# Queries that reach the scores' operands by DMA transpose alone, in a fused windowed attention and MLP kernel

## The chip, the core and the metric

The kernel runs on one core of a Trainium2 chip. The core has five engines with instruction streams of their own: TensorE (PE in the profile; its weight loads are PEld), VectorE (DVE), ScalarE (ACT), GpSimd (POOL) and SyncE (SP), which here only issues DMAs. Sixteen DMA engines move what is issued. On-chip memory has 128 partitions; PE reads it and writes to a separate accumulator memory (PSUM), which POOL does not read here.

The metric is the device time of one execution in microseconds (us), median over runs. The profile shows one execution, whose span runs from the first to the last instruction.

## The reference

Attention with a window of 32 positions to each side, for 8 batches of 8 heads, 576 positions of 64 numbers, followed by two matrix products with a leaky ReLU between them:

```python
B, H, S, D = q.shape                                   # 8, 8, 576, 64
scores = (1.0 / np.sqrt(D)) * np.matmul(q, k.transpose(0, 1, 3, 2))
mask = np.abs(pos[:, None] - pos[None, :]) <= 32
scores = np.where(mask, scores, -1e9)
attn = np.exp(scores - np.max(scores, axis=-1, keepdims=True))
attn = attn / (np.sum(attn, axis=-1, keepdims=True) + 1e-09)
o = np.matmul(attn, v)
x = o.transpose(0, 2, 1, 3).reshape(B * S, H * D)      # 4608 x 512
h = x @ w_in                                           # 512 x 2048
g = np.maximum(0.01 * h, h)
out = g @ w_out                                        # 2048 x 512, float32
```

All inputs and the output are float32; the kernel works in bfloat16 inside.

## The kernel before

**Tiling.** Heads are taken in pairs: a pair's two heads of 64 numbers fill the 128 partitions. There are 4 pairs a batch. Queries and keys must stand with the 64 numbers of a head along the partitions, so each pair's block of 96 partitions (positions) by 768 columns (6 runs of positions, 2 heads, 64 numbers) is cast to bfloat16 and transposed.

**Two ways through the attention.** Batches 0 and 1 (`BY_DMA = 2`) are transposed on PE (`transposes`, L321 to L346), 16 steps in all. Batches 2 to 7 are transposed by DMA (`transpose_dma`, L302): the queries into a tile `kT` and the keys straight into the scores' operand `kz`. The scores of these batches take a block of 128 keys and the queries of both heads at once (`score_blocks`, L369 to L385), so each head's queries must stand in their own 64 partitions with zeros in the other 64. That padded operand is `qz`, two planes of 576 columns a pair. The zero halves are cleared once (`clear_q`, L228 to L237: on DVE for the even batches' set, on ACT for the odd ones'), and `place_queries` (L314 to L319) copies each head's half from `kT` into its plane on DVE, two copies a pair, three steps after the cast.

**Memory.** Two sets (`sets`, L152) serve even and odd batches from 2 on; each holds `qz`, `kz` and `vw`, the values with columns of ones beside them, so that the product that weights the values also gives the sums (`product_blocks`, L387). `set_ones` (L239 to L252) writes the ones on DVE and zeroes two corners a pair on POOL. In batches 0 and 1 the same memory holds other operands, `qT`, `kbd`, `vbd`.

**Steps.** One call of `step` (L587) is one step of the attention: the scores two steps ahead (PE), their exponential (ACT, L382) and the band mask (POOL, L384, which writes `prob`), then `weighted`: the product of this step (PE, L395), two copies to `r` (ACT, L402 and L403), the reciprocal (DVE, L404) and the scaling into `xT` (DVE, L408). After that come the chores due: casts of queries and keys on POOL (`cast_qk`, L285), their transposes on SP (L305), casts of the values on POOL (`cast_vw`, L298 to L300), loads of the values (L116) and of the next batch's queries and keys (`load_qk`, L82 and L87), all issued on SP.

Steps 16 to 71 take four blocks of 64 positions of one pair; nine blocks make a batch. `base(b)` is the step at which batch b's scores are first used: 16, 24, 32, 40, 52 and 60. The scores themselves are made two steps before. Pair p of batch b is cast and transposed at step `base(b) + p - 7`, placed at `base(b) + p - 4`, and pair p of batch b + 1 is loaded at `base(b) + p - 4`. A pair's float32 tile has one buffer, so a load waits for the cast of the batch before.

**What sets the order.** The kernel's order is written out by hand. From step 8 on a list of due times (L766 to L776) puts the steps between the tiles of the two matrix products: `h_tile` (L500, out through ACT at L514) and `o_tile` (L549, out through ACT at L554 and a store on SP at L555). Every engine runs its instructions in the order in which the program issues them, and SP's queue holds loads, transposes and stores in that same order.

Of the kernel before, what the change touches and what calls it, by code (L numbers as in the profile page):

```python
# [10 lines left out]
BF16 = mybir.dt.bfloat16  # L11
AF = mybir.ActivationFunctionType
# [4 lines left out]
def kernel(  # L17
# [15 lines left out]
    nc = tc.nc  # L33

    B, H, S, D = q.shape
    W = 32
# [4 lines left out]
    NPAIR = H // 2  # L41
# [101 lines left out]
    nc.vector.memset(ones_bd[64:128, 64:128], 1.0)  # L143


    qb = const.tile([96, NPAIR, RUN, 2, D], BF16)
    kb = const.tile([96, NPAIR, RUN, 2, D], BF16)

    KPAD = S + 2 * W
    N_Q, N_K, N_V, N_BD = NPAIR * 2 * S, NPAIR * KPAD, NPAIR * NB * 3 * D, NPAIR * NB * 128  # L150
    N_SET = N_Q + N_K + N_V
    sets = [const.tile([128, N_SET], BF16, name=f"set{i}") for i in range(2)]  # L152
    qT, kbd, vbd, qz, kz, vw = [], [], [], [], [], []
    for t, at in zip(sets, (0, N_SET - NPAIR * S)):
        qT.append(sets[0][:, at:at + NPAIR * S].rearrange("p (n s) -> p n s", n=NPAIR))
# [27 lines left out]
        [((4, 0, 32), (6, 32, 64), (8, 96, 48)), ((5, 0, 64), (7, 64, 64))],  # L183
    ]

    win = const.tile([128, 2, 3, 64], BF16)
    nc.gpsimd.memset(win, 1.0)
    for lo in (0, 64):
        w = win[lo:lo + 64]
# [14 lines left out]
        lo = (16, 0)[hf]  # L204
        nc.gpsimd.tensor_copy(out=mask[hf][:, 1, :, lo:lo + 128], in_=win_f[:, :, 0:128])

    band = const.tile([128, 8, 2, 32], BF16)

    def make_band():

# [11 lines left out]
        yield  # L222

    band_parts = make_band()
    one = const.tile([128, 1], BF16)
    nc.vector.memset(one, 1.0)

    def clear_q(i, pairs, eng):  # L228
        for p in pairs:
            for a in range(2):  # L230
                r = slice(64 * (1 - a), 64 * (1 - a) + 64)
                if eng is nc.scalar:
                    eng.activation(
                        out=qz[i][r, p, a], in_=zero[r].to_broadcast([64, S]), func=AF.Copy)
                else:
                    eng.memset(qz[i][r, p, a], 0.0)
                yield  # L237

    def set_ones(i, pairs, eng):  # L239

        for p in pairs:
            to = vw[i][:, p, :, 1]
            if eng is nc.scalar:
                eng.activation(
                    out=to, in_=one.to_broadcast([128, NB * D]).rearrange("p (m d) -> p m d", d=D),
                    func=AF.Copy,
                )
            else:
                eng.memset(to, 1.0)
            nc.gpsimd.memset(vw[i][0:W, p, 0, 1], 0.0)  # L250
            nc.gpsimd.memset(vw[i][128 - W:128, p, NB - 1, 1], 0.0)
            yield  # L252

    def clear_k(i):
# [22 lines left out]


    def cast_qk(b, p, q_eng=None):
        for eng, src, dst in ((q_eng or nc.gpsimd, qf, qb), (nc.gpsimd, kf, kb)):  # L280
            to, tok = dst[:, p], src[b, p].rearrange("p a (c d) -> p c a d", d=D)
# [18 lines left out]
        nc.gpsimd.tensor_copy(out=to[64:128, 1::2, 0:3:2], in_=src[0:64, 1:5])  # L300

    def transpose_dma(b, p):  # L302
        t = kt.tile([128, S], BF16, name="kT")
        for to, src in ((t, qb), (kz[b % 2][:, p, W:W + S], kb)):
            nc.sync.dma_start_transpose(  # L305
                out=to.rearrange("p (c i) -> p c i", c=RUN),
                in_=src[:, p].rearrange("p c a d -> p (c a d)"),
            )
        landing.append((base(b) - 4 + p, b, p, t))

    def base(b):
        return OLD + NPAIR * (NB * (b - BY_DMA) // 4)

    def place_queries():  # L314
        while landing and landing[0][0] <= state["done"]:
            _, b, p, t = landing.pop(0)
            for a in range(2):
                r = slice(64 * a, 64 * a + 64)
                nc.vector.tensor_copy(out=qz[b % 2][r, p, a], in_=t[r])  # L319

    def transposes(b):  # L321

        for p in range(NPAIR):
            for which, src in (("q", qb), ("k", kb)):
                tp = mmps.tile([128, RUN, 96], BF16, name="tp", tag="mm")
                for c in range(RUN):
                    nc.tensor.transpose(  # L327
                        tp[:, c],
                        src[:, p, c].rearrange("p a d -> p (a d)"),
                        ident[0:96, 0:96],  # L330
                    )

                tok = tp.rearrange("p (e c) i -> p c i e", c=2)
                if which == "q":
                    nc.scalar.activation(
                        out=qT[b][:, p].rearrange("p (c i e) -> p c i e", c=2, e=RUN // 2),
                        in_=tok, func=AF.Copy,
                    )
                else:
                    kT = kt.tile([128, S], BF16, name="kT")  # L340
                    nc.scalar.activation(
                        out=kT.rearrange("p (i c) -> p i c", c=RUN),
                        in_=tp.rearrange("p c i -> p i c"), func=AF.Copy,
                    )
                    unplaced.append((b, p, kT))
                yield  # L346

    unplaced, landing = [], []

    def place_keys():  # L350

# [17 lines left out]
    def score_blocks(i):  # L369
        p, bs = i % NPAIR, blocks_of(i)  # L370
        n = 2 * 64 * len(bs)
        lo = 512 * (i % 2)
        sc = ps[:, lo:lo + n].rearrange("p (a w c i) -> p a w c i", a=2, c=2, i=32)
        for w, (b, m) in enumerate(bs):
            tok = qz[b % 2][:, p].rearrange("p a (g c i) -> p a g c i", c=2, i=96)
            at = 32 * (m % 3)
            nc.tensor.matmul(  # L377
                sc[:, :, w], kz[b % 2][:, p, 64 * m:64 * m + 128],
                tok[:, :, m // 3, :, at:at + 32], start=True, stop=True,
            )  # L380
# [200 lines left out]
    chores, more = [], []  # L581

    def chore(from_=chores):
        while from_ and next(from_[0], "end") == "end":
            from_.pop(0)

    def step():  # L587
        i = state["done"]
        if JOINED - 1 <= i < OLD - 1:
            join(i + 1)  # L590
        if i < NC - 2:
            score(i + 2)
        weighted(i)
        place_keys()
        place_queries()
        for b, p in qk_due.get(i, ()):
            cast_qk(b, p)
            transpose_dma(b, p)
        for b, p in v_due.get(i, ()):
            cast_vw(b, p)  # L600
        for b, p in v_next.get(i, ()):
            load_v_pairs(b, p)
        for b, p in qk_next.get(i, ()):
            load_qk(b, p)
        if i == 10:
            more.append(clear_q(1, range(NPAIR), nc.scalar))
        chore(more)
        if i == OLD - 2:
            chores.append(set_ones(0, (2, 3), nc.vector))
        if i == OLD:  # L610
            chores.extend([clear_k(1), set_ones(1, range(NPAIR), nc.vector)])
        if OLD - 6 <= i < OLD - 3:
            next(band_parts)
        chore()
        state["done"] += 1
# [95 lines left out]
    for f in range(4, FFC):  # L711
# [124 lines left out]
```

## Time and profile before

| | |
|---|---|
| median of 3 runs | 321.72 us (321.56 to 323.42) |
| the profiled execution | 321.12 us |
| its span | 319.4 us, TensorE clock granted in full |
| PE busy | 298.3 us |
| DVE busy | 227.3 us |
| ACT busy | 219.5 us |
| POOL busy | 200.1 us |
| DMA | 49.45 MB, mean 155 GB/s |
| L319, placing copies (DVE) | 48 of 487 ns, 23.4 us |
| L305, transposes (SP) | 48, of 1.2 us to issue (median) |

The page of the profile gives busy times, then the span in 40 slices of about 8 us, each digit the busy share in tenths. The list of waits says which engine waited at which line for whom: us in total, times, longest. The timeline gives instructions in order: start, duration, engine and line, operation, out<-in, count; "SPq" marks SP's issuing of DMAs, whose duration is the time to issue and not to land. A bracket at the end of a timeline row is idle time of the engine before it and what ended it. DMA shares count the packets' time against 16 engines, and go over 1 where packets of one engine overlap.

### The profile page before, as it was taken

The page shows a single profiled execution, that of the slowest core. Times are in us where ns is not written, and L with a number is a line of the kernel's source. Part 1 is how long each engine was busy: PE and PEld are TensorE (multiplying, and loading weights), DVE is VectorE, ACT ScalarE, POOL GpSimd, SP SyncE. Part 2 cuts the span into 40 slices and gives each one's busy share as a digit, 9 for nine tenths or more (in the row PEclk, how much of TensorE's full clock was granted, in tenths as well). Part 3 has the DMA queues.
Part 4 walks back from the last instruction along what each step waited for, and adds up shares of the span by engine and source line. Part 5 has one row for each costly group of instructions (what it writes and reads, how often), then busy time and mean ns, then how long its engine had stood idle before and what let it go on. Part 6 is the DMA issues. An engine that isn't in the chain of part 4 may idle for free.

```text
span 319.4 us, 6520 instructions
## 1 busy us (share of the span) xinstructions
PE 298.3 (93%) x2346; PEld 182.1 (57%) x2377; DVE 227.3 (71%) x299; ACT 219.5 (69%) x474; POOL 200.1 (63%) x262
## 2 busy tenths in 40 slices
PE   2678998999899899999999999999999999999995
PEld 1557774575665757676775555555555555544643
DVE  5688986899877997899779766787678766753000
ACT  7686689585865867776776975697569647842731
POOL 7899964997976987787677236678767722110000
PEclk9999999999999999999999999999999999999999
DMA  8999998998998699979969983699871011001001
GB/s 189 227 183 227 268 246 185 220 217 176 199 223 176 154 213 237 166 125 207 247 145 173 218 193 89 144 210 204 170 142 52 2 66 68 2 33 68 33 33 66
DMA packets 122416, 49.45 MB, mean 155 GB/s; under 512 B 96656, under 2 KB 117904, under 8 KB 122384
## 3 DMA queue, kind: packets, MB, share of 16 engines
q1 hardware_dynamic: 118160, 44.84, 68.5%
q0 software_dynamic: 4224, 4.19, 8.1%
q8 instruction: 18, 0.29, 0.4%
q14 instruction: 14, 0.11, 0.1%
HBM read 36.70 MB, written 9.44 MB: 144 GB/s over the span
## 4 chain that ended last, share of the span: by engine, by line
PE 76%; DVE 10%; ACT 5%; issue 4%; POOL 3%; DMA 1%; ACTq 0%; POOLq 0%; DVEq 0%
PE mm L549 34%; PE mm L500 32%; PE ps L377 3%; DVE r L404 2%; DVE set L319 2%; DVE r L451 2%; PE s L395 2%; PE x L395 1%; DVE xT L408 1%; DMA kT<-qb 1%; PE x L462 1%; PE ps L417 1%; PE tp L327 1%; PE s L446 1%; POOL prob L424 1%
## 5 line engine op out<-in xcount | busy, mean ns | idle before, releaser
L500 PE MATMUL mm<-xT,w_in_bf 128*128 128x288 bf16 (+3 forms) x824 | 134.7, 313 | 1.9 <-ACT gT L514 1.4
L549 PE MATMUL mm<-w_out_bf,gT 128*128 128x512 bf16 (+2 forms) x569 | 128.9, 373 | 1.3
L404 DVE RECIPROCAL r<-r 128x256 f32<-128x256 f32 (+1 forms) x56 | 95.0, 1696 | 37.7 <-ACT r L403 37.2
L500 PEld LDWEIGHTS <-w_in_bf 128*128 128x128 bf16 x832 | 79.0, 98 | 43.4 <-issue 2.9
L384 POOL TENSOR_TENSOR prob<-e,band 128x512 bf16<-128x512 bf16 (+1 forms) x56 | 62.7, 1119 | 63.1 <-ACT e L382 61.6
L514 ACT ACTIVATE gT<-mm 128x288 bf16<-128x288 f32 (+3 forms) x208 | 87.6, 469 | 15.7 <-PE mm L500 12.8
L549 PEld LDWEIGHTS <-gT 128*128 128x128 bf16 x592 | 55.0, 98 | 57.8
L382 ACT ACTIVATE e<-ps 128x512 bf16<-128x512 f32 (+1 forms) x56 | 32.5, 580 | 43.5 <-PE ps L377 35.8
L554 ACT ACTIVATE o_sb<-mm 128x512 f32<-128x512 f32 (+2 forms) x37 | 21.6, 585 | 24.1 <-PE mm L549 20.2
L451 DVE RECIPROCAL r<-s 128x288 f32<-128x288 f32 x16 | 31.2, 1951 | 4.4 <-PE s L446 4.0
L285 POOL CAST kb<-kf 96x768 bf16<-96x768 f32 x32 | 27.5, 862 | 4.1 <-DMA kf<-in_k_dram 4.0
L319 DVE COPY set<-kT 64x576 bf16<-64x576 bf16 x48 | 23.4, 487 | 3.9 <-DMA kT<-qb 3.1
L408 DVE TENSOR_TENSOR xT<-x,r 64x256 bf16<-64x256 f32 (+1 forms) x56 | 23.1, 413 | 3.3
L408 DVE TENSOR_TENSOR xT<-s,r 64x256 bf16<-64x256 f32 (+1 forms) x56 | 23.1, 413 | 3.3
L424 POOL TENSOR_TENSOR prob<-e,mask 128x576 bf16<-128x576 bf16 x16 | 20.4, 1274 | 7.3 <-ACT e L422 5.9
L377 PEld LDWEIGHTS <-set 128*128 128x128 bf16 x216 | 16.9, 98 | 13.0 <-issue 2.1
L377 PE MATMUL ps<-set 128*128 128x128 bf16 x216 | 22.0, 219 | 1.6 <-DVE set L319 1.5
L285 POOL CAST qb<-qf 96x768 bf16<-96x768 f32 x24 | 19.7, 821 | 0.0
L395 PEld LDWEIGHTS <-set 128*128 128x128 bf16 x432 | 17.9, 98 | 0.5
L298 POOL CAST set<-vbuf 128x640 bf16<-128x640 f32 x24 | 17.6, 732 | 0.0
L299 POOL CAST set<-vbuf 64x512 bf16<-64x512 f32 x24 | 14.7, 614 | 1.5
L300 POOL CAST set<-vbuf 64x512 bf16<-64x512 f32 x24 | 14.7, 612 | 1.2
(73 smaller groups left out, 220.6 us busy)
## 6 DMA issues: line engine op xcount, KB each, us to landing
qf<-in_q_dram SPq DMA_DIRECT2D x32, 288.0 KB, 5.3
kf<-in_k_dram SPq DMA_DIRECT2D x32, 288.0 KB, 6.1
out_dram<-o_sb SPq DMA_DIRECT2D x35, 256.0 KB, 2.5
vbuf<-in_v_dram SPq DMA_DIRECT2D x36, 128.0 KB, 4.4
vbuf<-in_v_dram SPq DMA_DIRECT2D x16, 144.0 KB, 6.2
vbuf<-in_v_dram SPq DMA_DIRECT2D x24, 96.0 KB, 4.1
w_in_bf<-in_moe_w_in_dram POOLq DMA_DIRECT2D x4, 512.0 KB, 8.5
w_out_bf<-in_moe_w_out_dram POOLq DMA_DIRECT2D x4, 512.0 KB, 16.4
```

The source lines that it names most:

```text
L285: eng.tensor_copy(out=to, in_=tok)
L319: nc.vector.tensor_copy(out=qz[b % 2][r, p, a], in_=t[r])
L377: nc.tensor.matmul(sc[:, :, w], kz[b % 2][:, p, 64 * m:64 * m + 128], tok[:, :, m // 3, :, at:at + 32], start=True, stop=True,)
L382: nc.scalar.activation(out=e[:, 0:n], in_=ps[:, lo:lo + n], func=AF.Exp, scale=scale)
L384: nc.gpsimd.tensor_mul(pr, e[:, 0:n], band.rearrange("p w c i -> p (w c i)")[:, 0:n])
L395: nc.tensor.matmul(x[:, a, w], vw[b % 2][:, p, m, a:a + 2].rearrange("p n d -> p (n d)"), pr[:, a, w], start=True, stop=True,)
L404: nc.vector.reciprocal(r[:, 0:n], r[:, 0:n])
L408: nc.vector.tensor_mul(xT[rows, p, t0:t0 + n], x[rows, a], r[rows, 0:n])
L451: nc.vector.reciprocal(r, s)
L500: nc.tensor.matmul(h[:, 0:n], w_in_bf[:, c, ts(f, 128)], xT[:, c, t0:t0 + n], start=(c == 0), stop=(c == DMC - 1),)
L514: nc.scalar.activation(out=to, in_=h, func=AF.Prelu, alpha=0.01)
L549: nc.tensor.matmul(o[:, lo:hi], gT[:, f, t0:t0 + 128], w_out_bf[:, f, lo:hi], start=(f == 0), stop=(f == FFC - 1),)
```

## The change

The queries of a pair are cast beside zeros. The buffer `qb` now has three slots instead of one place for each pair, and a slot has 1664 columns: head 0's six runs at columns 0 to 767, head 1's from 832 on, each run of 64 numbers followed or preceded by 64 columns of zeros. Seen as 12 blocks of 128 columns, the first six have head 0's numbers in the lower half and zeros above, the next six the reverse. One DMA transpose of 96x1536 then writes both padded planes of `qz`, zeros included. The slots are zeroed once (`clear_q`, six memsets on DVE: three in the second batch's first tiles, three at steps 9 to 11, since batches 0 and 1 use that part for plain casts).

Gone are `place_queries`, the clears of `qz`, the tile `kT` of the DMA's queries. Keys' casts have three slots too. Loads of pairs 2 and 3 come at `base(b) - 1` and `base(b) + 1` instead of `base(b) - 2` and `base(b) - 1`; as `base(b) + 1` is, for batches 2 to 4, also the step of the next batch's first transposes, pair 3's load now stands behind these in SP's queue. `set_ones` writes its corners on DVE, and for the first set all in the second batch's tiles. `qT` of batch 1 moves to the second set, the window's pattern and the band's mask into memory that is free at that time.

```diff
-    qb = const.tile([96, NPAIR, RUN, 2, D], BF16)
-    kb = const.tile([96, NPAIR, RUN, 2, D], BF16)
+    QB = 2 * RUN * 128 + 128
+    SLOTS = 3
+    qb = const.tile([96, SLOTS, QB], BF16)
+    kb = const.tile([96, SLOTS, RUN, 2, D], BF16)
+    qv = [
+        qb[:, p % SLOTS].rearrange("q (a x) -> q a x", a=2)[:, :, 0:RUN * 128]
+        .rearrange("q a (c e) -> q c a e", e=128)[:, :, :, 0:D]
+        for p in range(NPAIR)
+    ]
+    q01 = [
+        qb[:, p % SLOTS, 0:RUN * 128].rearrange("q (c a d) -> q c a d", a=2, d=D) for p in range(NPAIR)
+    ]
...
-        qz.append(t[:, 0:N_Q].rearrange("p (n a s) -> p n a s", n=NPAIR, a=2))
+        qz.append(t[:, 0:N_Q].rearrange("p (n s) -> p n s", n=NPAIR))
...
-    win = const.tile([128, 2, 3, 64], BF16)
+    win = sets[1][:, 0:384].rearrange("p (c m i) -> p c m i", c=2, i=64)
...
-    band = const.tile([128, 8, 2, 32], BF16)
+    band = mask[0].rearrange("p n c i -> p (n c i)")[:, 0:512].rearrange(
+        "p (w c i) -> p w c i", c=2, i=32)
...
-    def clear_q(i, pairs, eng):
...
+    def clear_q(p, a):
+        at = D if a == 0 else QB - 128 - RUN * 128
+        nc.vector.memset(
+            qb[:, p % SLOTS, at:at + RUN * 128].rearrange("q (c e) -> q c e", e=128)[:, :, 0:D], 0.0)
+
+    def set_ones(i):
+        for p in range(NPAIR):
+            nc.vector.memset(vw[i][:, p, :, 1], 1.0)
+            nc.vector.memset(vw[i][0:W, p, 0, 1], 0.0)
+            nc.vector.memset(vw[i][128 - W:128, p, NB - 1, 1], 0.0)
             yield
...
     def transpose_dma(b, p):
-        t = kt.tile([128, S], BF16, name="kT")
-        for to, src in ((t, qb), (kz[b % 2][:, p, W:W + S], kb)):
-            nc.sync.dma_start_transpose(
-                out=to.rearrange("p (c i) -> p c i", c=RUN),
-                in_=src[:, p].rearrange("p c a d -> p (c a d)"),
-            )
-        landing.append((base(b) - 4 + p, b, p, t))
+        nc.sync.dma_start_transpose(
+            out=qz[b % 2][:, p].rearrange("p (n i) -> p n i", i=96), in_=qb[:, p % SLOTS, 0:QB - 128],
+        )
+        nc.sync.dma_start_transpose(
+            out=kz[b % 2][:, p, W:W + S].rearrange("p (c i) -> p c i", c=RUN),
+            in_=kb[:, p % SLOTS].rearrange("p c a d -> p (c a d)"),
+        )
...
-    def place_queries():
-        while landing and landing[0][0] <= state["done"]:
-            _, b, p, t = landing.pop(0)
-            for a in range(2):
-                r = slice(64 * a, 64 * a + 64)
-                nc.vector.tensor_copy(out=qz[b % 2][r, p, a], in_=t[r])
...
-                qk_next.setdefault(base(b) + p - 4, []).append((b + 1, p))
+                qk_next.setdefault(base(b) + (-4, -3, -1, 1)[p], []).append((b + 1, p))
...
-        place_queries()
         for b, p in qk_due.get(i, ()):
+            if b == BY_DMA and p < SLOTS:
+                clear_q(p, 0)
             cast_qk(b, p)
             transpose_dma(b, p)
...
-        if i == 10:
-            more.append(clear_q(1, range(NPAIR), nc.scalar))
-        chore(more)
...
-    chores.extend([clear_q(0, range(NPAIR), nc.vector), clear_k(0),
-                   set_ones(0, (0, 1), nc.vector)])
+    chores.extend([clear_k(0), set_ones(0)])
...
+        if f < 4 + SLOTS:
+            clear_q(f - 4, 1)
```

More of the change, by code (lines that the diff above doesn't have):

```diff
@@ L153 @@
     qT, kbd, vbd, qz, kz, vw = [], [], [], [], [], []
-    for t, at in zip(sets, (0, N_SET - NPAIR * S)):
-        qT.append(sets[0][:, at:at + NPAIR * S].rearrange("p (n s) -> p n s", n=NPAIR))
+    for t in sets:
+        qT.append(t[:, 0:NPAIR * S].rearrange("p (n s) -> p n s", n=NPAIR))
         kbd.append(t[:, N_SET - 2 * N_BD:N_SET - N_BD].rearrange(
@@ L224 @@
     band_parts = make_band()
-    one = const.tile([128, 1], BF16)
-    nc.vector.memset(one, 1.0)
-    def clear_q(i, pairs, eng):
-        for p in pairs:
-            for a in range(2):
[L231 to L246, printed above, removed]
-                )
[L248 to L251, printed above, removed]
+    def clear_q(p, a):
[7 more added lines that the diff above has]
+            nc.vector.memset(vw[i][128 - W:128, p, NB - 1, 1], 0.0)
             yield
@@ L279, in cast_qk @@
     def cast_qk(b, p, q_eng=None):
-        for eng, src, dst in ((q_eng or nc.gpsimd, qf, qb), (nc.gpsimd, kf, kb)):
-            to, tok = dst[:, p], src[b, p].rearrange("p a (c d) -> p c a d", d=D)
+        for eng, src, dst in ((q_eng or nc.gpsimd, qf, (q01 if b < BY_DMA else qv)[p]), (nc.gpsimd, kf, kb[:, p % SLOTS])):
+            to, tok = dst, src[b, p].rearrange("p a (c d) -> p c a d", d=D)
             if eng is nc.scalar:
@@ L302, in transpose_dma @@
     def transpose_dma(b, p):
-        t = kt.tile([128, S], BF16, name="kT")
-        for to, src in ((t, qb), (kz[b % 2][:, p, W:W + S], kb)):
-            nc.sync.dma_start_transpose(
-                out=to.rearrange("p (c i) -> p c i", c=RUN),
-                in_=src[:, p].rearrange("p c a d -> p (c a d)"),
-            )
-        landing.append((base(b) - 4 + p, b, p, t))
+        nc.sync.dma_start_transpose(
[5 more added lines that the diff above has]
+        )
     def base(b):
         return OLD + NPAIR * (NB * (b - BY_DMA) // 4)
-    def place_queries():
-        while landing and landing[0][0] <= state["done"]:
-            _, b, p, t = landing.pop(0)
-            for a in range(2):
-                r = slice(64 * a, 64 * a + 64)
-                nc.vector.tensor_copy(out=qz[b % 2][r, p, a], in_=t[r])
     def transposes(b):
         for p in range(NPAIR):
-            for which, src in (("q", qb), ("k", kb)):
+            for which, src in (("q", q01[p]), ("k", kb[:, p % SLOTS])):
                 tp = mmps.tile([128, RUN, 96], BF16, name="tp", tag="mm")
@@ L328, in transposes @@
                         tp[:, c],
-                        src[:, p, c].rearrange("p a d -> p (a d)"),
+                        src[:, c].rearrange("p a d -> p (a d)"),
                         ident[0:96, 0:96],
@@ L346, in transposes @@
                 yield
-    unplaced, landing = [], []
+    unplaced = []
     def place_keys():
@@ L374, in score_blocks @@
         for w, (b, m) in enumerate(bs):
-            tok = qz[b % 2][:, p].rearrange("p a (g c i) -> p a g c i", c=2, i=96)
+            tok = qz[b % 2][:, p].rearrange("p (a g c i) -> p a g c i", a=2, c=2, i=96)
             at = 32 * (m % 3)
@@ L576 @@
             if b + 1 < B:
-                qk_next.setdefault(base(b) + p - 4, []).append((b + 1, p))
+                qk_next.setdefault(base(b) + (-4, -3, -1, 1)[p], []).append((b + 1, p))
             if b + 1 < B and p % 2 == 1:
                 v_next.setdefault(base(b) + p - 3, []).append((b + 1, p - 1))
-    chores, more = [], []
+    chores = []
     def chore(from_=chores):
@@ L604, in step @@
             load_qk(b, p)
-        if i == 10:
-            more.append(clear_q(1, range(NPAIR), nc.scalar))
-        chore(more)
-        if i == OLD - 2:
-            chores.append(set_ones(0, (2, 3), nc.vector))
         if i == OLD:
-            chores.extend([clear_k(1), set_ones(1, range(NPAIR), nc.vector)])
+            chores.extend([clear_k(1), set_ones(1)])
         if OLD - 6 <= i < OLD - 3:
```

## The prediction

> **What bounds the kernel now.** The page's first two parts come first: PE has 298.3 of 319.4 us busy, and the slices show it at 9 from the fifth slice on, the DMA engines at 8 or 9 through the first three quarters.
>
> ```profile
> PE 298.3 (93%) x2346; PEld 182.1 (57%) x2377; DVE 227.3 (71%) x299; ACT 219.5 (69%) x474; POOL 200.1 (63%) x262
> PE   2678998999899899999999999999999999999995
> DMA  8999998998998699979969983699871011001001
> ```
>
> So what an edit can win after the start is what PE idles there. PE's waits from 40 us on name it all:
>
> ```profile
> PE ps L377 <- DVE set L319: 1.5, 3, 0.7
> PE mm L500 <- ACT gT L514: 1.4, 3, 1.0
> PE x L462 <- ACT set L291: 1.1, 1, 1.1
> ```
>
> The reader sees 4.0 us. The change can touch the first row (scores waiting for placed queries, 0.63, 0.67 and 0.25 us at 106 to 115 us) and the 1.0 us of the second (at 86 us, where ACT is late by clears it no longer makes). All else that DVE and ACT are freed of lies beside a busy PE.
>
> Then the queue that feeds the scores, the timeline of SP:
>
> ```profile
> 88.50 0.51 SPq L87 DMA_DIRECT2D kf<-in_k_dram  x1
> 89.05 0.89 SPq L82 DMA_DIRECT2D qf<-in_q_dram  x1
> 89.98 1.15 SPq L87 DMA_DIRECT2D kf<-in_k_dram  x1
> 91.23 1.32 SPq L555 DMA_DIRECT2D out_dram<-o_sb  x1
> 92.64 4.35 SPq L116 DMA_DIRECT2D vbuf<-in_v_dram  x5
> 97.09 0.52 SPq L555 DMA_DIRECT2D out_dram<-o_sb  x1
> 97.71 1.23 SPq L305 DMA_TRANSPOSE kT<-qb  x1
> 99.05 1.21 SPq L305 DMA_TRANSPOSE set<-kb  x1
> 100.36 1.25 SPq L305 DMA_TRANSPOSE kT<-qb  x1
> ```
>
> The reader sees no gap between rows. SP issues with hardly a pause from 50 to 188 us: loads in a stretch where the DMA share is 1.07 to 1.11 (79 to 98, 109 to 126, 140 to 158 us), then a batch's eight transposes, 1.21 us each, with the share at 0.73 to 0.75 (98 to 109, 158 to 171; 0.99 in 126 to 140, where late loads were still landing). A plain DMA issues in as little as 0.31 us; so a transpose is bound by its issue, not by the engines that move it. The lag of this queue shows at its ends: the casts of batch 3's pair 0 ended at 88.9 us, their transpose left SP at 97.71; batch 4: 119.0 and 126.39; batch 5: 148.3 and 158.50. And there is almost no slack behind it: pair 0's keys land at 102.17 for scores that PE takes at 102.64 (batch 3), 131.67 for 133.36 (batch 4), 162.35 for 162.45 (batch 5). For batches 6 and 7 the slack is about 11 us or more (197.0 for 209.6; 229.9 for 240.9), and SP idles 4.8 us at 188.3.
>
> **The change part by part.**
>
> Removed on DVE: 48 placing copies x 487 ns = 23.4 us, 8 clears x 298 ns = 2.4 us. On ACT: 8 clears x 680 ns = 5.4 us. On POOL: 16 corner memsets x 0.14 us = 2.3 us, and its 5.8 us of waits for DVE before them. Added on DVE: 6 clears of 96x192 words (0.2 us by the 298 ns row of 288 words), 16 corners (0.07 us by the row of 16 words), 1.2 and 1.1 us. All this is beside PE except the 1.5 and 1.0 us above. The three clears at steps 9 to 11 stand behind the scaling at 59.7, 64.3 and 67.7 us, over before SP reaches the transposes (60.8, 67.1, 70.8), which wait for them: nothing. If that cover went, each would cost its 0.2 us.
>
> The 24 query casts on POOL (821 ns) write runs of 64 with gaps; the cast of values into strided places takes 732 ns for 640 elements, 1.14 ns each against 1.07, so about +0.05 us, hidden by POOL's 37% idle. Three slots make pair 3's cast wait for pair 0's transposes; these land at about 104 us, the pair's own load later (below), so that wait is hidden. The band in the mask's place and the window in the set's add nothing that is late.
>
> The 24 query transposes go from 6 blocks of 128 columns to 12, so that zeros move as data. No row shows such a size. Bounds: nothing more per issue, or twice 1.21, +1.21 us. I take the part above the least plain issue as growing with the columns: 1.21 - 0.31 = +0.90 us, near the upper end because the issue, not the data, is what takes the 1.21. Both ends stay for the range.
>
> A rule of the Trainium skill speaks the other way: "Advanced Engine Details and Errata", X-Bar Transpose (TRN2), has transpose DMAs as fast as regular ones. By it the larger one would issue like a plain load, at no added time (the first rival). The rows at 1.21 against 0.31 to 0.58 us speak against it, but none shows two sizes. "DMA: Bandwidth & Descriptors", in its comparison of issue times, has earlier generations push one command per tile, which agrees with a price by columns.
>
> Moved: pair 3's load goes behind pair 0's transposes of the same step. Ahead of them the queue loses the 2.13 us of 89.05 to 91.18 (batch 3), 1.56 (batch 4, 120.18 to 121.74) and 1.72 (batch 5, 150.73 to 152.45); behind them it gets 1.2 us (issues of 0.57 and 0.50). Pair 2's load, one step later, stands behind the same five value loads as before.
>
> Now the queue, shift by shift against before. Batch 2: the start at 60.78 is set by loads that stay. Four q transposes add 3.6; a gap of 0.46 at 69.9 takes some: the queue enters batch 3's loads 3.1 late. Pair 3's keys land at 83.9 for scores at 83.3, half a us that the saved 1.0 us at 86 pays.
>
> Batch 3: 3.1 - 2.1 = 1.0 late at pair 0; its own longer q adds 0.9, keys land at 102.17 + 1.9 = 104.1. PE, 0.5 ahead by then, stalls: shift +1.5. Pair 3's load now leaves at 102.2 and 102.8 and lands in 3.65 and 4.5 us (the rows at 79.43 and 80.06, on drained engines): 107.3. POOL works in order, its cast of that pair stood at 98.78, so it waits; the cast ends at 108.15, the probabilities behind it (1.15 us) at 109.3, and PE's product that reads them stood at 106.72: shift +2.6. The placing stalls of 0.67 and 0.25 go: +1.7. The queue leaves 1.0 + 3.6 + 1.2 = 5.8 late.
>
> Batch 4: 5.8 - 1.6 = 4.2 late. One key transpose there took 2.35 us right behind the loads; with a load fewer I drop its 1.1. Keys at 131.67 + 4.2 + 0.9 - 1.1 = 135.7 for 133.36 + 1.7: shift +2.3. Pair 3: load leaves by 134.7, lands 139.2, cast 140.0, probabilities 141.2 for a product at 137.50 + 2.3: +3.7, less 0.4 of placing stalls: +3.3. Queue 4.2 - 1.1 + 3.6 + 1.2 = 7.9 late.
>
> Batch 5: 7.9 - 1.7 = 6.2 late. Keys at 162.35 + 7.1 = 169.5 for 162.45 + 3.3: shift +7.0. Pair 3: load leaves by 168.7, lands 173.2, probabilities 175.2 for 166.65 + 7.0: +8.5. Batches 6 and 7 have the slack; PE is full there and gets nothing back. **Sum: +8.5 us on 321.1, the profiled execution's own time (0.6 under the median of 321.7): 329.6 us.**
>
> **The rivals.**
> *Issue hardly grows with columns, chance 0.28 for all that ends within 1% or faster.* Then the queue loses 2.1 ahead of each pair 0 and nothing is late: the saved 1.0, 1.5 and 0.4 us count, 318.2 us, on the other side of before. For: the half-idle engines in those stretches and the rule above; against: the even 1.21 us. With +0.90 costing 8.5 and 0 giving -2.9, the point is at about +0.25 us per transpose; below it faster. As even the whole saving is 0.9%, faster by over 1% needs more of ACT's and POOL's relief to reach PE: 0.07. Within 1% of 321.1, 317.9 to 324.3 (1% is about what a measurement can tell): 0.21.
> *Issue doubles in full, 0.15.* 0.31 us more on each of 13 query transposes up to batch 5's pair 0, 4.0 us: 333.6, and with loads landing at their medians of 5.2 and 6.0 us instead of 3.65 and 4.5, 1.5 more: 335.
> *The forecast, 0.57:* 324.3 to 332.5, the added price between 0.6 and 1.1 us. Were POOL's waits for pair 3's load covered, the last keys alone would set the shift, +7.0: 328.1.
> That the copies go is certain from the order of instructions; that the operand comes by DMA alone too.
>
> Slower by over 1% is 0.57 + 0.15 = 0.72. The range, 319.5 to 335, leaves out the faster case, the lowest of those within 1% (together 0.12) and what lies over the second rival's 335 (0.08).
>
> **What would show it.** Query transposes at about 2.1 us of issue on SP, keys' at 1.21; PE waiting at the scores' line for a DMA into the set around 104, 136 and 169 us; POOL waiting for pair 3's load in batches 3 to 5; no such waits after 190 us; DVE near 200 us busy. Wrong if query issues stay under 1.5 us, if SP shows gaps before the transposes (then it was not the bound and the shifts do not add up), or if the load stretches shrink when entered late.

## The result and the profile after

The changed kernel takes 323.53 us (median of 20 runs, 322.01 to 326.37) where the kernel before took 321.72 us beside it (20 runs, 320.27 to 323.42): a ratio of 1.0062, with a 95% interval of 1.0038 to 1.0086. It is slower by about 1.8 us, inside the bound of 1% that the prediction called no change, and the forecast of +8.5 us is four to five times too large. All but two of the runs below, one of twelve in each of two kernels, were in the faster of the two states in which executions come, and the ratios, which go by all of a kernel's runs and not by its median, leave those two out. The profiled execution took 324.62 us with a span of 322.9 us, 3.5 us over the profiled span before; why it shows twice the median's difference comes below.

The page of the changed kernel: busy times, and the slices for PE, for its granted clock and for the DMA engines.

```profile
PE 300.4 (93%) x2346; PEld 182.7 (57%) x2377; DVE 206.6 (64%) x264; ACT 215.7 (67%) x466; POOL 197.7 (61%) x246
...
PE   2678988999999799999999999999999999999995
...
PEclk9999999999999799999999999999999999999999
DMA  8999999998998999999999994898895011001001
```

DVE has lost 20.7 us and ACT 3.8 us, most of what the prediction took off them, and the time has not followed. The 14th slice (105 to 113 us) has a 7 in PE's row and in its clock's row, where before PE had an 8 and the full clock.

PE's waits from 40 us on (us in total, times, longest):

```profile
PE ps L367 <- DMA set<-kb: 3.2, 4, 2.1
...
PE mm L490 <- ACT gT L504: 0.3, 2, 0.2
...
PE s L385 <- POOL prob L374: 0.2, 1, 0.2
```

The scores (now L367) wait for a DMA of keys instead of for placing copies. ACT's 1.4 us at the first product (now L490) has become 0.3, the predicted relief. The third row is all that shows at PE of POOL's waiting for pair 3's load, for which the forecast had added 1.1 to 1.5 us in each of three batches. That POOL does wait there is in its own list, for 80 to 200 us:

```profile
POOL qb L282 <- DMA qf<-in_q_dram: 19.3, 5, 6.8
```

SP's queue around batch 3's transposes (queries L300, keys L303), the answer to the stretch shown of before:

```profile
98.29 1.39 SPq L300 DMA_TRANSPOSE set<-qb  x1
99.78 1.59 SPq L303 DMA_TRANSPOSE set<-kb  x1
101.42 0.57 SPq L82 DMA_DIRECT2D qf<-in_q_dram  x1
102.04 0.50 SPq L87 DMA_DIRECT2D kf<-in_k_dram  x1
102.65 2.40 SPq L300 DMA_TRANSPOSE set<-qb  x1
105.15 1.22 SPq L303 DMA_TRANSPOSE set<-kb  x1
106.46 1.32 SPq L300 DMA_TRANSPOSE set<-qb  x1
107.88 1.47 SPq L303 DMA_TRANSPOSE set<-kb  x1
```

A query transpose of 12 blocks takes 1.39 and 1.32 us to issue here, and 2.40 right behind the moved load; the key transpose behind it takes up to 1.59 instead of 1.21. Of all 24, 15 took 1.30 to 1.41 us and nine 1.92 to 2.68. From the query's start to the key's end a pair takes 3.31 us, mean of the 13 pairs up to batch 5's pair 0, against 2.77 before. So the size costs **0.54 us a pair, where the prediction priced it at 0.90**.

PE in the same stretch (a bracket is idle time before the row):

```profile
106.24 0.22 PE L367 MATMUL ps<-set 128*128 128x128 bf16 x1
108.53 0.34 PE L367 MATMUL ps<-set 128*128 128x128 bf16 x3 [2.07 <-DMA set<-kb]
108.71 0.40 PE L385 MATMUL s<-prob,set 128*128 128x64 bf16 x8
108.94 4.89 PE L490 MATMUL mm<-xT,w_in_bf 128*128 128x256 bf16 x28
```

The keys that PE waits for are those of pair 1, whose transpose left at 105.15 and landed at 108.48; the prediction had followed pair 0's. And the 28 matmuls behind the wait take 4.89 us; the same 28 took 3.35 us before. The clock's records show half the clock from 109.10 us on for 3.41 us. So this one wait moves PE by +1.44 and then +1.56 us. The product behind these scores (L385 at 108.71) needs probabilities that POOL finished at 108.46, late by its own wait for pair 3's load: two waits ended together here, and with the keys in time PE would still have waited till about 108.5. Both go back to a queue that was late.

PE's shift against before, start of matmul against start of matmul, stands at +1.4 by 47 us and at +1.7 by 85. From there it moves in steps: -1.2 at 87 (ACT's clears are gone); +1.4 at 108.5 and +1.6 up to 113 (the half clock); -0.8 and -0.4 at 114 and 117 (the placing stalls are gone); +0.6 at 147; +0.3 and +0.4 at 170. At the end it stands at +3.5.

### The profile page after: what moved, and what is told of

Same layout as the page of the kernel before. It is cut to its first block, busy times and chain, and to the rows that moved or that the text cites. A ratio compares the mean times of both kernels' runs of the same rounds, so it can differ in the third digit from the quotient of the medians.

```text
span 322.9 us, 6463 instructions
## 1 busy us (share of the span) xinstructions
PE 300.4 (93%) x2346; PEld 182.7 (57%) x2377; DVE 206.6 (64%) x264; ACT 215.7 (67%) x466; POOL 197.7 (61%) x246
## 4 chain that ended last, share of the span: by engine, by line
PE 53%; DMA 9%; POOL 4%; SPq 3%; ACT 2%; issue 2%; ACTq 0%; POOLq 0%
PE mm L539 24%; PE mm L490 24%; DMA set<-kb 4%; DMA kf<-in_k_dram 3%; PE ps L367 3%; POOL prob L374 2%; DMA set<-qb 1%; PE s L385 1%; PE x L385 1%; DMA qf<-in_q_dram 1%; SPq L303 1%; POOL set L295 1%; SPq L116 1%; SPq L300 1%; POOL set L297 1%
## 5 line engine op out<-in xcount | busy, mean ns | idle before, releaser
L490 PE MATMUL mm<-xT,w_in_bf 128*128 128x288 bf16 (+3 forms) x824 | 135.8, 316 | 0.9 <-ACT gT L504 0.3
L490 PEld LDWEIGHTS <-w_in_bf 128*128 128x128 bf16 x832 | 79.9, 99 | 42.6 <-issue 1.2
L504 ACT ACTIVATE gT<-mm 128x288 bf16<-128x288 f32 (+3 forms) x208 | 88.8, 469 | 18.3 <-PE mm L490 14.7
L374 POOL TENSOR_TENSOR prob<-e,mask 128x512 bf16<-128x512 bf16 (+1 forms) x56 | 62.7, 1120 | 51.6 <-ACT e L372 49.8
L367 PEld LDWEIGHTS <-set 128*128 128x128 bf16 x216 | 16.7, 98 | 15.0 <-DMA set<-kb 4.3
L367 PE MATMUL ps<-set 128*128 128x128 bf16 x216 | 21.9, 219 | 3.3 <-DMA set<-kb 3.2
L385 PEld LDWEIGHTS <-set 128*128 128x128 bf16 x432 | 18.0, 98 | 0.8 <-issue 0.4
L412 ACT ACTIVATE e<-ps 128x576 bf16<-128x576 f32 x16 | 10.4, 652 | 4.0 <-PE ps L407 3.9
```

The lines of the kernel that those rows point to most:

```text
L367: nc.tensor.matmul(sc[:, :, w], kz[b % 2][:, p, 64 * m:64 * m + 128], tok[:, :, m // 3, :, at:at + 32], start=True, stop=True,)
L385: nc.tensor.matmul(x[:, a, w], vw[b % 2][:, p, m, a:a + 2].rearrange("p n d -> p (n d)"), pr[:, a, w], start=True, stop=True,)
L490: nc.tensor.matmul(h[:, 0:n], w_in_bf[:, c, ts(f, 128)], xT[:, c, t0:t0 + n], start=(c == 0), stop=(c == DMC - 1),)
L504: nc.scalar.activation(out=to, in_=h, func=AF.Prelu, alpha=0.01)
```

## The experiments

Every ratio is against the kernel before, run on the same chip, with a 95% interval.

### One part alone: the loads spread, the queries placed as before

```diff
 # the kernel before
-                qk_next.setdefault(base(b) + p - 4, []).append((b + 1, p))
+                qk_next.setdefault(base(b) + (-4, -3, -1, 1)[p], []).append((b + 1, p))
```

> The kernel before, with only its loads spread as in the change. Transposes stay at 6 blocks and the queries are placed on DVE. Theory A (SP's queue): pair 0's transposes of batch 3 leave 2 us earlier, near 95.6 us; pair 1's about 1 us earlier; the placing stalls of 1.2 us do not grow; 321 to 322 us, within 0.3% of before. Rival B (POOL's waits for pair 3's load reach PE): POOL waits 4 us or more in each of three batches and PE waits for prob, 323 us or more.

Measured: 320.75 us (9 runs), ratio 0.9951 (0.9930 to 0.9972), faster than both kernels. Batch 3's first transpose leaves SP at 96.63 us instead of 97.71, half of the 2 us expected, and no wait of PE for placed queries over 0.12 us is left. POOL waits 11.3 us for pair 3's loads, and none of it reaches PE. So the move of the loads is the good part of the change, and what I feared of it does not happen.

### The other part alone: padded transposes, the loads where they were

```diff
 # the changed kernel
-                qk_next.setdefault(base(b) + (-4, -3, -1, 1)[p], []).append((b + 1, p))
+                qk_next.setdefault(base(b) + p - 4, []).append((b + 1, p))
```

> The changed kernel, with the loads of queries and keys at the steps of before, so that pair 3's load stands ahead of pair 0's transposes again. Theory A (SP's queue sets the scores of batches 3 to 5; a load ahead of the transposes delays them by its 1.6 to 2.1 us): pair 0's keys of batch 3 land about 1.9 us later than the 102.7 of the changed kernel, PE waits about 1.5 us for pair 0 instead of 2.1 us for pair 1, POOL's 21 us of waits for loads go; 323 to 324.5 us. Rival B (POOL's waits for pair 3's load are the loss): 321.5 us or less.

Measured: 327.42 us (4 runs), ratio 1.0160 (1.0131 to 1.0189). Both forecasts missed it: without the spread the padded kernel is 5.5 us slower than the kernel before, not 1.8. PE's waits from 40 us on:

```profile
PE ps L367 <- DMA set<-kb: 4.0, 4, 1.8
PE mm L490 <- ACT gT L504: 1.3, 2, 1.1
PE mm L490 <- ACT o_sb L544: 1.2, 1, 1.2
```

POOL's, from 80 to 200 us:

```profile
POOL qb L282 <- DMA set<-qb: 15.7, 3, 6.2
```

The queue is later (batch 3's first transpose leaves at 100.72), and the keys with it. The other two rows of PE are a second victim of the same queue: at 157 to 161 us ACT waits 3.60 us for an output store that stands behind loads. POOL's 15.7 us is the third slot: pair 3's cast waits for pair 0's transpose. Whether that wait costs time this run cannot tell; a later one can.

### The price doubled: each query transpose as two

```diff
 # the changed kernel
-        nc.sync.dma_start_transpose(
-            out=qz[b % 2][:, p].rearrange("p (n i) -> p n i", i=96), in_=qb[:, p % SLOTS, 0:QB - 128],
-        )
+        for a in range(2):
+            nc.sync.dma_start_transpose(
+                out=qz[b % 2][:, p, a * S:a * S + S].rearrange("p (n i) -> p n i", i=96),
+                in_=qb[:, p % SLOTS, a * RUN * 128:(a + 1) * RUN * 128],
+            )
```

> The changed kernel, with each padded query transpose issued as two of 6 blocks: the same bytes, the same result, and the full price of a second issue, 1.2 to 1.3 us a pair, which was my upper end. In the changed kernel the one transpose of 12 blocks issued in 1.3 us where nothing stood ahead of it. Theory A (the issue on SP is what reaches PE, my sum with the smaller price): about 0.85 us more for each pair's queries and keys than the changed kernel's 2.9 us; pair 0's keys of batches 3, 4 and 5 land about 4, 7 and 10 us later; 328 to 331 us. Rival B (the queue has room that I did not see): within 1 us of the changed kernel's 323.5 us.

Measured: 336.14 us (5 runs), ratio 1.0430 (1.0399 to 1.0460). PE's waits from 40 us on:

```profile
PE ps L369 <- DMA set<-kb: 12.9, 8, 2.9
```

SP at batch 3's first pair (the two halves, then the keys):

```profile
101.15 2.54 SPq L301 DMA_TRANSPOSE set<-qb  x2
103.78 1.22 SPq L305 DMA_TRANSPOSE set<-kb  x1
```

Query and key now take 4.39 us a pair (mean of the first 13), +1.62 on before, and the time is up by 14.2 us, more than either forecast: key waits of 2.9, 3.5, 4.5 and 1.9 us in batches 2 to 5, and in the profiled execution two stretches of half clock. The same blocks in two issues cost far more than in one, so the price goes by issues first and by blocks second.

### The disputed cost by itself: transposes alone

Attention and matrix products are left out; the kernel only zeroes a buffer, sends transposes of 96 partitions in various sizes, some behind four loads of 288 KB, and stores the zeros.

```diff
+    for sizes in ((3,) * 6, (6,) * 6, (12,) * 6, (24,) * 4, (12, 6, 12, 6, 12, 6)):
+        for i, n in enumerate(sizes):
+            turn(i, n)          # one transpose of n blocks of 96x128
+        drain(len(sizes))
...
```

> The disputed price by itself: no attention and no products (the output is zeros), only DMA transposes of 96 rows from SP, in groups of one size (3, 6, 12 and 24 blocks of 128 columns), 12 and 6 in turn, and groups behind four plain loads. Theory A (a transpose's issue grows with its columns, but a few blocks' worth is taken in at once and SP only waits when more is outstanding): 6 blocks at 1.21 us each; the first of 12 blocks at about 1.3 us, later ones back to back near 2.2 to 2.4 us; 12 and 6 in turn about 2.9 us a pair; behind loads 2.3 to 2.7 us for 12. Rival B (12 blocks cost 1.3 us however they are stacked, and the loads alone make 2.4 of it): 1.3 us each in the group of 12.

Measured, on SP (groups of 3, 6, 12 and 24 blocks, then 12 and 6 in turn; then 12, 6, 6 behind four loads; last four loads and 12, 12, 6 behind them):

```profile
23.29 7.74 SPq L35 DMA_TRANSPOSE t<-wide  x6
35.78 7.78 SPq L35 DMA_TRANSPOSE t<-wide  x6
48.49 9.63 SPq L35 DMA_TRANSPOSE t<-wide  x6
63.72 12.15 SPq L35 DMA_TRANSPOSE t<-wide  x4
81.48 8.69 SPq L35 DMA_TRANSPOSE t<-wide  x6
...
105.75 4.83 SPq L35 DMA_TRANSPOSE t<-wide  x3
116.27 1.79 SPq L32 DMA_DIRECT2D ld<-in_q_dram  x4
118.11 6.12 SPq L35 DMA_TRANSPOSE t<-wide  x3
```

Divided by the count: 1.29, 1.30, 1.61 and 3.04 us; 12 and 6 in turn 2.90 a pair. Three blocks cost as much as six, so **there is a floor of about 1.3 us an issue, and only above six blocks does the size show**, by 0.12 us a block from 12 to 24. A second six blocks cost 0.3 us (2.90 against 2 x 1.30), not 0.90. That lies between the two forecasts: for 12 blocks back to back the theory had 2.2 to 2.4 us and the rival 1.3. Behind four loads 12, 6 and 6 took 4.83 us and 12, 12 and 6 took 6.12 (1.48, 3.27 and 1.27): there six more blocks cost 1.29 us, a full issue.

What sets in above six blocks shows in the DMA engines' share, in a stretch within each of the first four groups (each row: the stretch, its length, DVE and POOL busy, clock, DMA share, GB/s):

```profile
25.00:31.00 6.00, 0.68 (x5) 0.00 (x0) 1.00 0.25 50
38.00:44.00 6.00, 0.78 (x5) 0.00 (x0) 1.00 0.57 111
51.00:58.00 7.00, 0.63 (x4) 0.00 (x0) 1.00 0.92 173
66.00:76.00 10.00, 0.47 (x3) 0.00 (x0) 1.00 1.03 194
```

With 3 and 6 blocks the engines are a quarter and half busy, and the issue is what limits; with 12 they are nearly full and with 24 full. In the two groups behind loads the share is 1.05 (105.7 to 110.6 us) and 1.16 (118.1 to 124.2). So the part that grows goes with full engines: SP then most likely waits for the data to move, and no longer for its own issuing. No run separates the two.

### The size taken away, all else kept

The query transpose moves six blocks into the first plane only. The second head's queries are left out from batch 2 on: their plane is zeroed once a set, by four memsets on DVE.

```diff
 # the changed kernel
-            out=qz[b % 2][:, p].rearrange("p (n i) -> p n i", i=96), in_=qb[:, p % SLOTS, 0:QB - 128],
+            out=qz[b % 2][:, p, 0:S].rearrange("p (n i) -> p n i", i=96), in_=qb[:, p % SLOTS, 0:RUN * 128],
...
```

> The changed kernel, but the query transposes move only the first six blocks (96x768), into the first plane; the second plane is zeroed once for each set by four DVE memsets of 128x576, and the slots' second clear goes. The scores of the second head's queries are left out in effect (their plane holds zeros from batch 2 on); every engine does the same work as in the changed kernel. Theory A (what the padded queries cost is the larger transposes' time in SP's queue, as the bare issue measurement gave it: 1.31 against 1.57 to 1.69 us, and up to 2.7 behind loads): the key waits at the scores' line go, and the time falls to that of the kernel before with its loads spread: 319.8 to 321.5 us, ratio 0.993 to 0.999. Rival B (the cost is in the rest that came with them: three slots in which casts wait for transposes, POOL's casts into gaps, the clears beside POOL's early casts): the waits go, but the time stays between 322.5 and 324, ratio 1.002 to 1.007.

> The same with the loads of pairs 2 and 3 back at the steps they had before; again the second head's queries are left out from batch 2 on. With 12 blocks this placing of the loads took 327.4 us, 5.5 more than the kernel before. Theory A (size of the transposes): most of the 5.5 goes, 321.0 to 322.8 us; what stays is the early shift of 0 to 1.5 us. Rival B (three slots: pair 3's cast waits for pair 0's transposes, which POOL showed with 15.7 us): POOL still waits some 10 to 15 us for the slot, and PE for probabilities behind it, 324.5 to 327 us.

> The changed kernel itself, beside the two others on the same chip, so that they are compared with it directly: 322.5 to 325 us, ratio 1.004 to 1.009. Theory and rival say the same here. It also tells whether half a granted clock of 3.4 us behind PE's wait for keys at 106 to 109 us comes again: if it belongs to that wait, in every profile with a wait of 2 us there; if it is a chance of one execution, not.

Measured on one chip: with six blocks 319.74 us (6 runs), ratio 0.9928 (0.9907 to 0.9949); the same with the loads back 321.35 us (12 runs), 0.9958 (0.9934 to 0.9981); the changed kernel itself 324.95 us (9 runs), 1.0070 (1.0042 to 1.0097), a little above its 323.53 of the first comparison, with the intervals overlapping. SP with six blocks and the loads spread, at the same place as above:

```profile
94.92 1.24 SPq L303 DMA_TRANSPOSE set<-qb  x1
96.26 1.75 SPq L306 DMA_TRANSPOSE set<-kb  x1
98.06 0.57 SPq L82 DMA_DIRECT2D qf<-in_q_dram  x1
98.69 0.50 SPq L87 DMA_DIRECT2D kf<-in_k_dram  x1
99.29 1.72 SPq L303 DMA_TRANSPOSE set<-qb  x1
101.11 1.22 SPq L306 DMA_TRANSPOSE set<-kb  x1
```

PE in the same kernel, the 28 matmuls that took 4.89 us:

```profile
107.31 3.35 PE L493 MATMUL mm<-xT,w_in_bf 128*128 128x256 bf16 x28
```

The first pair leaves 3.4 us earlier than in the changed kernel, pair 1's keys land at 104.41 instead of 108.48, PE waits for no keys, and the 28 matmuls take 3.35 us again. So the six more blocks cost 5.2 us beside the spread (3.8 if the changed kernel's first median, from another chip, is taken), and 6.1 without it (327.42 less 321.35, across two chips). They take bytes out of the DMA engines as well as time out of SP's queue, and this run does not tell those apart. All the rest together, the copies and clears gone, the three slots, the casts into gaps, the spread, gains 0.7%, where the spread alone gained 0.5%. POOL's 15.7 us of waiting for a slot are 10.9 us with the loads back and six blocks, and that kernel is still faster than before: the rival that blamed the slots falls. (That profile is of the slowest of its twelve runs, 326.39 us, in which ACT's wait for a store held PE for 2.90 us; the median does not rest on that run.)

### An early shift that looked like the change's

PE's first +1.4 us, at 43 to 47 us, comes with DVE's cast of the second batch's queries, 1.75 us in the changed kernel against 0.56 before. I suspected the ones that `set_ones` now writes in those tiles, and held them back:

```diff
 # the changed kernel, second batch's tiles
-        chore()
+        if f > 11:
+            chore()
```

> The changed kernel, with the ones of the first set written after the second batch's casts and keys instead of between them. In the profiles PE stood 1.3 us later from 43 to 46 us on, where DVE ran three ones with their corners (0.7 us each) ahead of the keys' placing and the next query cast. Theory A (DVE's order in the second batch costs 1.3 us of the loss): 1.3 us faster than the changed kernel, 322.2 us, PE's shift against before at 47 us under 0.3 us, everything behind it as in the changed kernel. Rival B (the early shift is eaten later, since the transposes' landing sets PE at batch 3 anyway): about 323.2 us, the shift at 47 us gone but the wait for keys at 106 us longer by about as much.

Measured: 325.86 us (6 runs), ratio 1.0101 (1.0074 to 1.0127): no gain. The early shift is gone (+0.12 at 47 and at 51 us), and the scores wait for keys instead, all the longer:

```profile
PE ps L367 <- DMA set<-kb: 5.2, 7, 1.6
```

Pair 1's keys of batches 3, 4 and 5 land 1.5, 1.3 and 0.9 us earlier than in the changed kernel, but PE stands up to 3.0 us earlier (1.6 of that because no half clock came here) and waits for most of the difference: 0.6 us of the lead is left in the profiled execution, and none in the median. So what was won ahead of the queue was for the most part paid back at the queue. Nor does such a shift need the change: the kernel before with its loads spread, where nothing in that part differs, showed 3.21 us for that cast and a shift of +1.7 at 47 us in its profile.

### Loads of values out of the queue's way

```diff
 # the changed kernel; then the same edit on the kernel before, with and without the spread
-                v_next.setdefault(base(b) + p - 3, []).append((b + 1, p - 1))
+                v_next.setdefault(base(b) + p + 1, []).append((b + 1, p - 1))
```

> The changed kernel, with the next batch's values loaded four steps later, behind pair 1's and pair 3's transposes instead of ahead of all of them. Nothing else moves. Theory A (what stands ahead of the transposes in SP's queue is what makes PE wait): pair 0's transposes of batch 3 leave when their cast is done, near 91 us instead of 98.3, those of batches 4 and 5 near 122 and 152; PE's waits for keys go (3.2 us in the changed kernel's profile), POOL's waits for pair 3's load fall under 5 us; 319.0 to 320.5 us. Rival B (DMA engines are full and values landing later hold up POOL's casts of them instead): POOL waits for vbuf and PE for prob, 322 us or more.

> The kernel before with only the values four steps later. Theory A: pair 0's transposes of batch 3 leave about 5 us earlier, placing stalls go, 320 to 321 us, like the spread alone (320.75). Rival B (only pair 3's place in the queue matters): 321.5 to 322 us.

> The kernel before with both moves of loads, queries' and keys' spread as in the change and values four steps later, and the queries still placed on DVE. Theory A: no wait for a placed query is left, 1.2 us against the spread alone or a little less: 319.3 to 320.5 us. Set beside the changed kernel with late values it tells what the padded transpose is worth once the queue has room: the same within 0.5 us if the removed copies were beside PE all along, up to 1 us slower if ACT's clears (1.0 us of waiting at 86 us) count.

Measured: on the changed kernel 329.44 us (5 runs), ratio 1.0222 (1.0196 to 1.0248); on the kernel before 320.58 us (12 runs), 0.9953 (0.9934 to 0.9972); with the spread as well 321.05 us (12 runs), 0.9965 (0.9942 to 0.9988). In the changed kernel with this edit, PE's waits from 40 us on:

```profile
PE x L385 <- POOL prob L374: 6.1, 3, 2.5
PE ps L367 <- DMA set<-kb: 1.5, 3, 0.6
```

POOL's, from 80 to 200 us:

```profile
POOL set L295 <- DMA vbuf<-in_v_dram: 25.3, 7, 5.6
```

The transposes leave early (90.85 us), the key waits fall by half, and the values land late in their place, as the rival had it: POOL waits for them with the probabilities queued behind. This is the stall that the prediction feared of pair 3's loads, with its mechanism right and its place wrong. With plain queries the same edit wins 0.5%: POOL waits for values there too, 17.7 us from 80 to 200 us, but PE has no wait for probabilities. The two good edits do not add, against the forecast.

## Why the prediction was wrong, point by point

**What bounds the kernel: right.** PE is full, SP's queue sets when keys land, and nearly every wait of PE after 80 us stands at the scores' line and is for keys. (It called a transpose bound by its issue and not by the engines that move it. At six blocks that holds, at a share of 0.57; at twelve the share is 0.92.)

**The price of a query transpose, +0.90 us: the step that failed.** It split 1.21 us into 0.31 of fixed cost, the issue of a plain load, and 0.90 that grows with the columns. The bare measurement shows the opposite split: about 1.3 us at three blocks and at six, so nearly all of it is fixed, and 0.3 us for the next six. In the kernel it was +0.54 us a pair, since nine of the 24 cost more, most of them close behind loads. "Wrong if query issues stay under 1.5 us" was met by 15 of them (1.30 to 1.41 us) and not by these nine (1.92 to 2.68 us).

**The ledger, given a price: roughly right in its total.** Of its 8.5 us, 5.8 were waits for keys, 4.0 waits for probabilities behind pair 3's load, and 1.3 came off as gains; what came, as steps of PE's shift, was the early 1.4, 2.6 at keys, 1.6 of half clock, which the ledger did not have, and 0.4 at probabilities, with 2.4 off as gains. Its own ends are -2.9 us at no price and +8.5 at 0.90, which is 12.7 us of time for each us of price. By that line +0.54 gives +4.0, where the profiled execution has +3.5 and the median +1.8; six blocks (2.72 us a pair, a price of -0.05) give -3.5, measured -2.4; two transposes (+1.62) give +17.7, measured +14.2. The sign turns between a price of 0 and 0.5, as the break-even of 0.25 said, but the slope measured is nearer to 10 (16.6 us from six blocks to two transposes).

**Lags: a quarter to three fifths as large.** Pair 0's transposes were forecast 1.0, 4.2 and 6.2 us late in batches 3 to 5, and were 0.6, 1.1 and 1.7. Besides the price, batch 4's loads took 14.4 us in the queue instead of 17.4, half of which the ledger had not seen: its own sign of being wrong, a stretch of loads that shrinks when entered late, was met in that batch. Batch 3's stretch (16.2 us) and batch 5's (16.0) are as forecast.

**Keys: the wrong pair.** Pair 0's keys of batch 3 landed at 102.7, in time; those of pair 1, which now stand behind the moved load and its slow query transpose, were 2.07 us late, and the ledger had not followed them. By its own prices they would have landed at 108.3 (104.27 + 1.0 + 0.9 + 1.2 + 0.9), and they landed at 108.48. In batch 5 the keys cost 0.3 us instead of 3.7.

**POOL's waits for pair 3's load: right in place, wrong in price.** They are there (6.78 us before the cast at 105.52, 5.48 before the one at 135.89). The load had landed at 106.4 instead of 107.3, the probabilities behind it were done at 108.46, and PE was held by keys until 108.53. So in batch 3 this wait was hidden behind the other and not absent; in batch 5 0.2 us of it showed. In the kernel before with spread loads, where the same load left 2.2 us earlier, none did.

**Gains: nearly right.** 1.2 us at 87 us (forecast 1.0) and 0.8 and 0.4 at 114 and 117 (forecast 0.67 and 0.25). The 0.4 forecast for batch 4 has no row: the kernel before has no placing stall there. DVE came to 206.6 us, not near 200.

**Rivals.** "Issue hardly grows" was given 0.28, and what came lies in its band, though by a price between the two cases. The rule behind it (the Trainium skill, "Advanced Engine Details and Errata", X-Bar Transpose (TRN2), transposes as fast as regular DMAs) does not hold for the issue: 1.29 us for three blocks against 0.31 to 0.58 for a load of 288 KB. Nor does it hold for the data here: with the engines full the transposes of 24 blocks moved 194 GB/s, and the plain store at the end of the same run up to 389.

What stays open: why some of the larger transposes close behind loads take 1.9 to 3.3 us and others 1.3 (right behind five loads of values at 160.24 us, for one) is not explained beyond the full engines; and the changed kernel's two medians are 1.8 and 2.8 us above the kernel before, with ratios whose intervals overlap and runs that scatter from 322.0 to 326.4 in the first comparison alone, of which the clock, below, explains a part.

## What to carry to other kernels

A cost in a queue has a fixed and a growing part, and one row at one size cannot tell them apart: bound the split from both sides, and let it decide the forecast only when a second size is seen. In a queue that feeds the bounding engine, follow every item behind a moved one and not only the first, and expect most of the time won ahead of it to be paid back at it. Work moved from an engine with slack into such a queue is no gain, though the engine's busy time falls by 20 us; here the same edits without the larger transfer (and without the second head's queries, so no kernel to keep), and a mere reordering of loads, were both faster.

## What the hardware showed that I had not expected

**A wait of 2.07 us cost 1.5 us more than itself.** The granted clock fell to half for 3.413 us (once for twice that) behind PE's longest waits, and not behind shorter ones. Once more the changed kernel, in the later comparison, and the kernel with later values:

```profile
109.08 0.34 PE L367 MATMUL ps<-set 128*128 128x128 bf16 x3 [2.50 <-DMA set<-kb]
109.26 0.47 PE L385 MATMUL s<-prob,set 128*128 128x64 bf16 x8
```

```profile
152.36 0.59 PE L385 MATMUL x<-prob,set 128*128 128x64 bf16 x8 [2.54 <-POOL prob L374]
...
186.18 0.39 PE L385 MATMUL x<-prob,set 128*128 128x64 bf16 x8 [1.91 <-POOL prob L374]
```

Half clock followed at 109.45 and at 152.38 us, and none followed the wait of 1.91: there the eight products take 0.39 us, against 0.59 at half clock. Cut each profile into windows of 3.413 us from its first clock record, and add up PE's idle time in each: the six windows between 45 and 300 us with 2.07 us or more (2.07, 2.41, 2.50, 2.54, 2.90 and 2.94, in five of the kernels above) were each followed by half clock, and no window with 1.93 or less was. The borders matter: with the loads back, 2.24 us of idle within 3.4 us cost nothing, as a border divided it and neither part passed 1.7.

The Trainium skill, "TensorE: Matmul & The Clock Gate", has such free-running windows in Part 1, and the length agrees; its rule of no idle gaps over about 3 us is too mild for these rows, in which 2.07 us was enough. The clock is also a likely part of why the profiled execution lost more than the median: its mean clock is 0.995, as in 3 of the first comparison's 20 runs (324.62 to 326.25 us), and 13 of them show 1.000 (median 323.67). It is not the whole: in the later comparison runs at 1.000 took up to 325.31 us beside 325.18 and 325.21 at 0.995.

**A floor for transposes by DMA, and what comes above it.** Three blocks issue no faster than six; a transpose that is split pays the floor twice, while in one issue the second six blocks cost a quarter of it. Above the floor the DMA engines are nearly full, at 173 to 194 GB/s, about half of what the plain store reached.
